# Sliding-window attention with an S4 convolution: the softmax's maximum over eight keys, one reduction in PSUM or three two-operand maxima on a bf16 copy

## The chip, the cores and the metric

The kernel runs on one core of a Trainium2 chip. The metric is the device time of one execution in microseconds (us); lower is better. A profile of one execution gives each engine's instructions with their times, counted from the start of the span. The engines are PE (TensorE, the matmuls; PEld is its weight loads), DVE (VectorE), ACT (ScalarE), POOL (GpSimd) and SP (SyncE, which here issues the DMAs). Each engine works through its own instructions in order and waits on semaphores for the others.

## The reference, cut to what matters

Four layers follow one another on x of shape 1 x 2048 x 512, each added to its own input: attention A, convolution B, attention A, convolution B. The attention has 32 heads of 16 channels, and each position sees only eight keys: itself and those 2, 4, ... 14 positions back.

```python
W, dil = 8, 2
idx = pos[:, None] - off[None, :]          # off = arange(8) * 2
logits = einsum("bhsd,bhswd->bhsw", q, kg) * scale
logits = where(mask, logits, -1e9)         # mask: idx >= 0
attn = softmax(logits, axis=-1)            # over the 8 keys w
o = einsum("bhsw,bhswd->bhsd", attn, vg)
x = x + o.reshape(B, S, D) @ wo            # A, on layernorm(x)
x = x + irfft(rfft(u) * rfft(K)) + u * Dskip   # B, u = layernorm(x); ...
```

The softmax's maximum over the eight keys is what the change touches. Any number near the maximum gives the same softmax up to rounding, since it is subtracted from all eight logits.

## The kernel before

Sequence positions are laid out as 16 rows of 128 partitions (position = 16 p + row), so that a shift by two positions is a shift by two rows. The attention is the method `core` (from L307), called once per attention layer (l = 0 and 1). It has two parts that run into each other.

The **logit part** goes over four blocks q of four rows each and over four quarters ft of the channels. `mult` (L295, DVE) writes the products of q with eight shifted k as prod, 128 x 4096 bf16, in two buffers. `lsum` (L302, PE) sums groups of 16 channels with 32 small matmuls into the PSUM tile L of the block, 128 x (4 rows, 8 keys, 32 heads) in f32; after the last quarter `mask` (L285, PE) adds -1e9 where a key lies ahead of the sequence. L has two buffers. Then the softmax of the block:

- `mx` (L365, DVE): one tensor_reduce over the keys, which reads L from PSUM with the keys as the innermost, strided axis, and writes mx, 128 x 128 bf16.
- `sub_exp` (L372, PE, and L375, ACT): two matmuls with the negative identity subtract mx inside L, and one activation writes ex = exp(scale * L) as 128 x 1024 bf16 to SBUF.
- `recip` (L382, PE; L384 and L386, ACT): sums ex over the keys by eight matmuls, then takes ln and exp(-.) of the sum, giving rs.
- `norm_p` (L392, DVE): attn = ex * rs.

Between these, PE computes the projections `q_proj` (L185) and `v_proj` (L351), which ACT copies out of PSUM (L187 and L353). Once all odd or all even rows of v are there, two DMAs shift them by one partition (L356, L357).

The **PV part** goes over the 16 rows n. `pv_mult` (L402, DVE) writes attn times eight shifted v as pav (128 x 4096 bf16, two buffers); `pv_sum` (L412, PE) sums and transposes it with 64 matmuls into po (one PSUM buffer), which ACT copies to oT (L415); `out_proj` (L424, PE) follows one row later, and ACT writes the new x_sb with its sum (L430) and the sum of its squares (L108, into ln_junk). Each of these two ends in an accumulator read. The layernorm of the next layer is begun and applied in between (L133 to L160). The last block's logits are still made during this part: its four `mult` come after n = 1, 3, 5 and 7, so block 2's maximum falls at n = 0 and block 3's at n = 8.

In layer 0 ACT and DVE also prepare the convolution during the PV part: sines for a table (L700, with a table load before and after, L700 and L1367), and the copies k_perm from k_rl (L1354).

The order on DVE, ACT, PE and SP is the program's own within the attention. The counts n and ft, and a dictionary `ev` keyed by places such as ("p", 8), say where in the loops the other work goes:

```python
for n in range(16):
    pv_mult(rows[n])
    if n in (0, 8):
        mx(2 + n // 8)
    ...
    event(("p", n))
    ...
    pv_sum(rows[n])
    if n in (0, 8):
        sub_exp(2 + n // 8)
```

The convolution is the class FftB: its constant g_sb (1 MB) is loaded by SP (L726), as are the filter's spectra into kf_ring (L795, L797) and kx in its second pass. Its first step is the matmuls L756. These loads stand outside the written order: where they go on SP depends on when the memory that they overlay comes free.

Of the kernel before, what the change touches and what calls it, by code (L numbers as in the profile page):

```python
# [20 lines left out]
P = 128  # L21
# [42 lines left out]
u m UA m u m u m u m u u yD yA u m yA m m u u u m yA m yA  # L64
yA m yD yD yA yD yA yA yA yD z01D z03D yA yA z00D z02D z12D z11A z10D z13B
"""

def build_a_consts(tc, nc, cpool, tpool):
    c = {}
# [93 lines left out]
class LayerA:  # L163
# [125 lines left out]
    def mult(self, q, ft, pr=None):  # L289
        nc, a0, kT = self.nc, q * 4, self.kT  # L290
        if pr is None:
            pr = self.prp.tile([P, W, 4, P], BF16, name="prod")[:]
        kb = kT[:, ft, a0 + 14: a0 + 18, :]
        kap = bass.AP(tensor=kT.tensor, offset=kb.offset, ap=[list(kb.ap[0]), [-2 * P, W], [P, 4], [1, P]])
        nc.vector.tensor_tensor(pr, self.qT[q][:, ft].unsqueeze(1).to_broadcast([P, W, 4, P]), kap, ALU.mult)  # L295
        self.st[q][ft] = pr
# [7 lines left out]
        if ft == NDT - 1:  # L304
            self.mask(q)

    def core(self, x_sb, u, lnp, ev=None, nprod=0):  # L307

        tc, nc, lnst, l = self.tc, self.nc, self.lnst, self.layer
        ident, nident = self.c["ident"], self.c["nident"]  # L310
        scale = float(DH) ** -0.5
        xnT = self.xnT
        ev = ev or {}
        if self.ps_l is None:
            self.open_logits()
        st, linit, mult, lsum = self.st, self.linit, self.mult, self.lsum

        def event(key):
            for f in ev.get(key, ()):
                f()  # L320

        with ExitStack() as c2:
            big = c2.enter_context(tc.tile_pool(name=f"a{l}_big", bufs=1, reuse_waits="tile"))
# [24 lines left out]
            def v_proj(a):  # L348
                pp = pq_tile()
                for dt in range(NDT):  # L350
                    nc.tensor.matmul(pp[:], lhsT=xnT[:, dt, a * P:(a + 1) * P],  # L351
                                     rhs=wv[:, dt, :], start=(dt == 0), stop=(dt == NDT - 1))
                nc.scalar.copy(v[:, 14 + a, :].rearrange("p (d h) -> p d h", h=H), pp[:].rearrange("p (h d) -> p d h", h=H))  # L353
                if a >= 14:
                    b = a - 14
                    nc.sync.dma_start(v[1:113, b:14:2, :], v[0:112, 16 + b:30:2, :])  # L356
                    nc.sync.dma_start(v[113:128, b:14:2, :], v[112:127, 16 + b:30:2, :])  # L357
                    if b + l == 0:
                        self.load_wo(big)
                    event(("v", b))  # L360

            def mx(q):
                L = st[q]["L"]
                m = wk.tile([P, 4, H], BF16, name="mx", bufs=1)
                nc.vector.tensor_reduce(m[:], L[:].rearrange("p a w h -> p a h w"), AX.X, ALU.max)  # L365
                st[q]["mx"] = m

            def sub_exp(q):
                L, m = st[q]["L"], st[q]["mx"]
                ex = wk.tile([P, 4, W, H], BF16, name="ex", bufs=1)  # L370
                for j in range(2):
                    nc.tensor.matmul(L[:, 2 * j:2 * j + 2], lhsT=nident[:],  # L372
                                     rhs=m[:, 2 * j:2 * j + 2].unsqueeze(2).to_broadcast([P, 2, W, H]),
                                     start=False, stop=True, skip_group_check=True)
                nc.scalar.activation(ex[:], L[:], ACT.Exp, scale=scale)  # L375
                st[q]["ex"] = ex

            def recip(q):
                ex, L = st[q]["ex"], st[q]["L"]
# [69 lines left out]
            def u_end(a0):  # L449
                lns[a0] = ln_end(nc, lnp, lns[a0])  # L450

            def u_apply(a0, rows, eng=None):
                rstd, nb = lns[a0]
                for a in rows:
# [2 lines left out]

            nc.sync.dma_start(v[0:1, 0:14, :].rearrange("p a (n c) -> p (a n) c", c=64),
                              self.c["zrow"].unsqueeze(1).to_broadcast([1, 112, 64]))
            projs = [(q_proj, 1, ft) for ft in range(NDT)] if 1 not in self.qT else []  # L460
            vs = [*range(0, NA, 2), *range(1, NA, 2)]
            projs += [(v_proj, a) for a in vs[:6]] + [(q_proj, 2, ft) for ft in range(NDT)]
            projs += [(v_proj, a) for a in vs[6:]]
            slots = [(0, ft) for ft in range(nprod, NDT)] + [(q, ft) for q in (1, 2) for ft in range(NDT)]
            free = 2 if l else 0
            lead = 0 if l else 2
            per, acc = (len(projs) - lead) / (len(slots) - free - 0.5), float(lead)

            def proj(n):
                nonlocal acc  # L470
                acc += n
                while acc >= 1 and projs:
                    f, *args = projs.pop(0)
                    f(*args)
                    acc -= 1

            for q, ft in slots:
                if q == 1 and ft == 0 and 1 not in self.qT:
                    while 1 not in self.qT or projs[0][0] is q_proj:
                        proj(1)  # L480
                event(("m", q, ft))
                mult(q, ft)
                event(("q", q, ft))
                if ft == 0:
                    linit(q)
                if q or ft >= free:
                    proj(per)
                if ft == 0 and q > 0:
                    mx(q - 1)
                lsum(q, ft)  # L490
                if ft == 0 and q > 0:
                    proj(0.5)
                    acc -= 0.5
                    sub_exp(q - 1)
                if ft == 2 and q > 0:
                    recip(q - 1)
                if ft == 3 and q > 0:
                    norm_p(q - 1)
            proj(100)
            linit(3)  # L500
            q_proj(3, 0)
            rows = [0, 2, 1, *range(3, NA)]
            for n in range(16):
                pv_mult(rows[n])
                if n in (0, 8):
                    mx(2 + n // 8)
                if n in (2, 10):
                    recip(2 + n // 8)
                if n in (4, 11):
                    norm_p(2 + n // 8)  # L510
                if n in (1, 3, 5, 7):
                    mult(3, n // 2)
                if n in (7, 11, 15):
                    u_begin(n - 7, n - 3, "act", "act" if n > 7 else "pool")
                if n in (8, 12):
                    u_end(n - 8)
                if n in (9, 10, 13, 14):
                    b0 = 0 if n < 11 else 4
                    r0 = b0 + (0 if n in (9, 13) else 2)
                    u_apply(b0, range(r0, r0 + 2))  # L520
                if n == 15:
                    x_stats(12)
                event(("p", n))
                if n in (1, 3, 5):
                    q_proj(3, n // 2 + 1)
                pv_sum(rows[n])
                if n in (0, 8):
                    sub_exp(2 + n // 8)
                if n == 15:
                    x_stats(13)  # L530
                    if l == 1:
                        u_end(8)
                        u_apply(8, range(8, 12), "dve")
                if n > 0:
                    out_proj(rows[n - 1])
                if n in (1, 3, 5, 7):
                    lsum(3, n // 2)
                event(("o", n))
            if l == 0:
                out_proj(15)  # L540
                return {"a": lambda: [u_end(8), u_apply(8, range(8, 12), "pool")], "s": lambda: x_stats(14), "t": lambda: x_stats(15),
# [744 lines left out]
def kernel(  # L1286
# [74 lines left out]
    with tc.tile_pool(name="ctmp_g2", bufs=1) as g2tmp, tc.manual_schedule(engines=MAN):  # L1361
        gx, gs = build_g2(nc, g2tmp, C["p21"], g2_dram, kp[:].rearrange("p q a r -> p (q a r)"))
        G = lambda f, h: lambda: f(h)
        K = lambda h, j: lambda: k_part(h, j)
        ev = {("v", 0): [lambda: x_load((0,))], ("v", 1): [lambda: x_load((1, 2, 3))], ("o", 1): [lambda: k_half_load(0)], ("o", 2): [G(gs, 0)], 
              ("m", 0, 3): [G(gx, h) for h in range(4)],
              ("p", 3): [G(gs, 1)], ("p", 4): [G(gs, 2)], ("p", 5): [G(gs, 3), lambda: k_half_load(1)], ("o", 5): [lambda: nc.scalar.preload_act_table_set(EXP_LN)],  # L1367
              ("p", 6): [lambda: k_half_fix(0), K(0, 0)], ("p", 7): [K(0, 1)], ("p", 8): [lambda: la.load_w2(w2_dram), K(0, 2)], ("p", 9): [K(0, 3)],
              ("p", 12): [lambda: k_half_fix(1), K(1, 0)], ("p", 13): [K(1, 1), K(1, 2)], ("p", 14): [K(1, 3)]}
        late = la.core(x_sb, u, lnp, ev, 3)  # L1370
    late["m"] = C["masks"]
    krctx2.close()
    la.close_logits()
# [13 lines left out]
    with tc.manual_schedule(engines=MAN):  # L1387
# [33 lines left out]
        fb.c_ps.close()  # L1421
        fb.c_grp.close()
        krctx.close()
        ev = {("p", 8): [lambda: la.load_w2(w2_dram)]}
        ev["m", 0, 0] = [last(("P", 3, 0), ("P", 3, 1), ("x", 0), ("x", 2), ("P", 3, 2), ("Q", 0, 1), ("e", 0), ("Q", 0, 2))]
        ev["m", 0, 1] = [last(("e", 1), ("e", 2))]
        ev["m", 0, 2] = [last(("e", 3))]
        ev["q", 0, 0] = [last(("P", 3, 3), ("Q", 0, 3))]
        la.core(x_sb, u, lnp, ev)
    la.close_logits()  # L1430

    fb = FftB(tc, nc, C, consts["ident"], w2_dram, g2_dram, kf_dram, x_sb, 1)
# [47 lines left out]
```

## Time and profile before

| what | us |
|---|---|
| median of 3 runs | 422.05 |
| lowest and highest | 421.33 and 422.5 |
| the profiled execution's own time | 418.89 |
| its span in the profile | 417.1 |
| logit part of layer 0 and of layer 1, about | 104 to 140 and 276 to 312 |
| PV part of layer 0 and of layer 1, about | 140 to 196 and 312 to 365 |
| second convolution, about | 369 to 417 |

The span is what lies between the first and the last instruction that the profile shows; the execution's own time is 1.79 us longer. A line of a timeline gives the start, the duration, the engine, the source line, the operation, what it writes and reads with shapes, and how many instructions were merged into the line; a bracket at its end gives how long the engine was idle before it and what it waited for. A line of a group gives the count, the busy time in us and the mean of one in ns, and then the idle time before such instructions.

### The profile page before, as it was taken

The numbers are of one execution on the slowest core, as the hardware profiler recorded it, in microseconds if no ns is written. First come the engines' busy times: TensorE is split into PE (matmuls) and PEld (weight loads), VectorE is DVE, ScalarE is ACT, GpSimd is POOL, SyncE is SP. The second block draws the span as 40 slices with busy tenths as digits, with TensorE's granted clock in tenths as the row PEclk, the third lists the DMA queues.
The fourth block names the chain that finished last, engine by engine and source line by source line (L and its number), as shares of the span: only waits on it lengthen the run. The fifth ranks groups of instructions, "written<-read, shape, count | busy, mean of one in ns | idle before, by whom it ended". The sixth has DMA issues, their size and how long they took to land.

```text
span 417.1 us, 15864 instructions
## 1 busy us (share of the span) xinstructions
PE 320.5 (77%) x7048; PEld 231.5 (55%) x7106; DVE 387.9 (93%) x515; ACT 321.7 (77%) x552; POOL 37.7 (9%) x46
## 2 busy tenths in 40 slices
PE   3000068999999987778998779999998978896885
PEld 2000036667756565556887768555665655566774
DVE  8999999999899999996999969979779999989995
ACT  6999998987445569987999998863555758779972
POOL 3000200000396000000500000000000020000000
PEclk9999998999999999999999999999999999999899
DMA  8940642113014666393226597730043027504506
GB/s 222 383 125 13 73 90 71 33 40 89 14 40 123 179 180 189 99 389 109 70 89 229 217 306 218 231 99 2 3 114 89 5 79 328 156 3 140 168 10 197
DMA packets 62462, 54.36 MB, mean 130 GB/s; under 512 B 33877, under 2 KB 50874, under 8 KB 61114
## 3 DMA queue, kind: packets, MB, share of 16 engines
q1 hardware_dynamic: 62250, 53.22, 42.0%
q8 instruction: 55, 0.90, 0.9%
q10 hardware_dynamic: 144, 0.13, 0.1%
q14 instruction: 13, 0.11, 0.1%
HBM read 30.28 MB, written 13.24 MB: 104 GB/s over the span
## 4 chain that ended last, share of the span: by engine, by line
PE 35%; DVE 21%; ACT 14%; issue 5%; DMA 5%; SPq 3%; DVEq 0%; ACTq 0%
PE pq L351 6%; DVE pav L402 5%; DVE t L805 5%; PE L L302 4%; DVE a1s L745 4%; PE pk L1175 4%; PE pq L185 3%; DVE prod L295 3%; PE pp L242 3%; PE po L412 3%; PE pp L1113 3%; PE pq L424 2%; SPq L1280 2%; DMA w_sb<-w_dram 2%; ACT ub L818 1%
## 5 line engine op out<-in xcount | busy, mean ns | idle before, releaser
L402 DVE TENSOR_TENSOR pav<-attn,v_ext 128x4096 bf16<-128x4096 bf16 x32 | 72.8, 2283 | 0.1
L295 DVE TENSOR_TENSOR prod<-qT,kT_ext 128x4096 bf16<-128x4096 bf16 x29 | 66.0, 2299 | 3.9 <-PE L L302 3.8
L412 PE MATMUL po<-ident,pav 64*128 64x64 bf16 x2048 | 36.3, 190 | 15.1 <-DVE pav L402 7.7
L412 PEld LDWEIGHTS <-pav 64*128 64x128 bf16 x2048 | 32.5, 95 | 26.0 <-DVE pav L402 14.9
L1103 PE MATMUL pt<-ident,x_blk 128*128 128x128 bf16 x64 | 7.0, 260 | 43.4 <-ACT x_blk L158 43.4
L1015 DVE TENSOR_TENSOR A_t<-A_t,pow_t 128x1024 bf16<-128x1024 bf16 (+4 forms) x46 | 38.1, 868 | 0.2
L424 PE MATMUL pq<-wop,oT 128*128 128x512 bf16 x121 | 31.7, 379 | 4.3 <-issue 3.8
L353 ACT CAST v_ext<-pq 128x512 bf16<-128x512 f32 x32 | 18.8, 587 | 19.2 <-PE pq L351 17.5
L818 ACT CAST ub<-pb 128x1024 bf16<-128x1024 f32 x32 | 32.2, 1036 | 1.7 <-DVE t L805 0.8
L763 PE MATMUL pb<-a1s,w_sb 128*128 128x64 bf16 x768 | 28.4, 196 | 6.2 <-ACT a1s L745 2.9
L302 PEld LDWEIGHTS <-prod 128*128 128x128 bf16 x928 | 27.0, 96 | 8.1 <-DVE prod L295 2.5
L1103 PEld LDWEIGHTS <-x_blk 128*128 128x128 bf16 x64 | 5.4, 117 | 46.1 <-ACT x_blk L158 44.4
L745 DVE CAST a1s<-pb 128x1024 bf16<-128x1024 f32 x23 | 27.0, 1215 | 3.9 <-PE pb L756 3.9
L763 PEld LDWEIGHTS <-w_sb 128*128 128x128 bf16 x768 | 25.8, 100 | 8.6 <-issue 6.8
L351 PE MATMUL pq<-wv,xnT 128*128 128x512 bf16 x118 | 29.9, 379 | 0.5
L1113 PE MATMUL pp<-xnT,kT_ext 128*128 128x512 bf16 x87 | 25.0, 406 | 6.2 <-ACT qT L1118 3.3
L302 PE MATMUL L<-ind,prod 128*128 128x8 bf16 x928 | 27.4, 166 | 0.8 <-DVE prod L295 0.6
L415 ACT CAST oT<-po 128x512 bf16<-128x512 f32 x32 | 18.5, 577 | 11.5 <-PE po L412 11.2
L745 ACT CAST a1s<-pb 128x1024 bf16<-128x1024 f32 x25 | 24.9, 1034 | 2.5 <-PE pb L756 2.2
L1175 PEld LDWEIGHTS <-A_t 128*64 128x64 bf16 (+1 forms) x512 | 22.3, 105 | 3.6
L1175 PE MATMUL pk<-B_t,A_t 128*64 128x84 bf16 (+1 forms) x512 | 24.1, 203 | 0.1
L832 PE MATMUL pb<-Wp,t 64*128 64x64 bf16 x512 | 19.4, 192 | 5.9 <-ACT ub L818 2.8
(225 smaller groups left out, 809.8 us busy)
## 6 DMA issues: line engine op xcount, KB each, us to landing
w_sb<-w_dram SPq DMA_DIRECT2D x8, 1024.0 KB, 9.4
w_dram<-w_zero SPq DMA_DIRECT2D x1, 4096.0 KB, 14.8
kf_ring<-kf_dram SPq DMA_DIRECT2D x13, 256.0 KB, 3.7
kf_ring<-kf_dram SPq DMA_DIRECT2D x26, 128.0 KB, 3.6
v_ext<-v_ext SPq DMA_DIRECT2D x4, 784.0 KB, 6.2
x_blk<-in_A_x_dram SPq DMA_DIRECT2D x4, 512.0 KB, 4.1
kT_ext<-in_A_wqkv_dram SPq DMA_DIRECT2D x4, 512.0 KB, 10.1
x_sb<-in_A_x_dram SPq DMA_DIRECT2D x4, 512.0 KB, 5.4
```

Of the source, the lines that this page charges most:

```text
L295: nc.vector.tensor_tensor(pr, self.qT[q][:, ft].unsqueeze(1).to_broadcast([P, W, 4, P]), kap, ALU.mult)
L302: self.nc.tensor.matmul(L[:, al, w, ft * 8:(ft + 1) * 8], lhsT=pr[:, w, al, :], rhs=self.c["ind8"][:], start=(ft == 0 and w == 0 and al % ...
L351: nc.tensor.matmul(pp[:], lhsT=xnT[:, dt, a * P:(a + 1) * P], rhs=wv[:, dt, :], start=(dt == 0), stop=(dt == NDT - 1))
L402: nc.vector.tensor_tensor(pv[:], attn[:, n % 4].unsqueeze(2).to_broadcast([P, W, DH, H]), vap, ALU.mult)
L412: nc.tensor.matmul(po[:, h, 0, ft, :], lhsT=pvf[rows, w, ft * P:(ft + 1) * P], rhs=ident[rows, rows], start=(w == 0 and ft == 0), stop=(w ...
L424: nc.tensor.matmul(pw[:], lhsT=oT[:, ftp, :], rhs=self.wo[:, ftp, :], start=False, stop=(ftp == NDT - 1))
L745: (self.nc.scalar.copy if eng == "act" else self.nc.vector.tensor_copy)(dst, src)
L763: nc.tensor.matmul(p2[:, j, :], lhsT=self.w2[:, ec * EC + j, :], rhs=a1s[:, ec * EC + j, :], start=True, stop=True)
L818: nc.scalar.copy(ub[:], p2)
L1015: return lambda: nc.vector.tensor_tensor(*args)
L1113: nc.tensor.matmul(pps[kind, b, ft][:], lhsT=la.wqk[:, dt, c:c + P], rhs=la.xnT[:, dt, b * 512:(b + 1) * 512], start=(dt == 0), stop=(dt = ...
L1175: nc.tensor.matmul(o, lhsT=lhs, rhs=Bt[:, ri, c * CH + ql].rearrange("p b g -> p (b g)"), start=(not half and j % 4 == 0 and ri == 0), sto ...
```

## The change

The maximum is no longer taken from PSUM. A new step `lcopy` has ACT copy the masked logits L to bf16 in SBUF, into the tile that will later hold ex. `mx` then takes the maximum over the keys with three tensor_tensor instructions in place: keys 0 to 3 against 4 to 7 (512 results per partition), then 0 and 1 against 2 and 3 (256), then 0 against 1 (128 results, into mx). `sub_exp` still subtracts mx from the f32 logits in PSUM and still writes ex, over the copy. The tile ex gets two buffers in place of one.

```diff
+            def lcopy(q):
+                L = st[q]["L"]
+                ex = wk.tile([P, 4, W, H], BF16, name="ex", bufs=2)
+                nc.scalar.copy(ex[:], L[:])
+                st[q]["ex"] = ex
 
             def mx(q):
-                L = st[q]["L"]
+                ex = st[q]["ex"]
                 m = wk.tile([P, 4, H], BF16, name="mx", bufs=1)
-                nc.vector.tensor_reduce(m[:], L[:].rearrange("p a w h -> p a h w"), AX.X, ALU.max)
+                for n in (4, 2, 1):
+                    o = ex[:, :, 0:n] if n > 1 else m[:].unsqueeze(2)
+                    nc.vector.tensor_tensor(o, ex[:, :, 0:n], ex[:, :, n:2 * n], ALU.max)
                 st[q]["mx"] = m
 
             def sub_exp(q):
-                L, m = st[q]["L"], st[q]["mx"]
-                ex = wk.tile([P, 4, W, H], BF16, name="ex", bufs=1)
+                L, m, ex = st[q]["L"], st[q]["mx"], st[q]["ex"]
...
                 nc.scalar.activation(ex[:], L[:], ACT.Exp, scale=scale)
-                st[q]["ex"] = ex
```

The loops and events of `core` are replaced by a string for each layer that names one operation per letter, in the order in which they are issued (m mult, l lsum, q and v the projections, c lcopy, x mx, e sub_exp, r recip, n norm_p, P pv_mult, S pv_sum, O out_proj, b, d and a the layernorm, digits and capitals the convolution's preparation):

```diff
+CORE0 = """
+0mvvvvlcmvvxlemqqlmqqlrmvvlcnmvvxlvemvlmvvlrmvvlcnqPxSePmqSOl1PrSO2Pm3qSOlPn4SOPm56qSOl7P8ASOPmb
+BSOlcPxdwCSeOPaaDSOPraaSOPnbSOPd9ESOPaaFGSOPaaHSOPbtStO
+"""
+CORE1 = """
+0m1l2ml3mqqlmqqvlcmvvxlvemvvlmqqlrmqqvlcnmvvxlvemvvlmvvlrmvvlcnqPxSePmqSOlPrSOPmqSOlPnSOPmqSOlPS
+OPmbSOlcPxdwSeOPaaSOPraaSOPnbSOPdSOPaaSOPaaSOPbtStdaaaaO
+"""
```

In the built programs the instructions of PE and POOL stand in the same order before and after. On DVE each tensor_reduce is replaced by three tensor_tensor at its place, and nothing else moves. On ACT each lcopy is put in right after the block's last `lsum` and `mask` in the order of issue: in layer 0 behind the fourth v_ext copy, then between others of them, before the first qT copy of the PV part, and, for block 3, between an accumulator read of ln_junk and a k_perm copy (the letters `lcPxdwC`). On SP the second g_sb load stands behind the kx loads in place of ahead of the ring's first loads, and one pair of ring loads (L797) stands ahead of the first v_ext shift of layer 1 in place of behind it.

More of the change, by code (lines that the diff above doesn't have):

```diff
@@ L66 @@
 """
+CORE0 = """
[6 more added lines that the diff above has]
+"""
+ROWS0 = (0, 2, 1, 3, 4, 5, 6, 7, 8, 9, 10, 11, 12, 13, 14, 15)
+ROWS1 = (0, 2, 1, 3, 4, 5, 6, 7, 8, 9, 10, 11, 12, 13, 14, 15)
+VROWS = (*range(0, 16, 2), *range(1, 16, 2))
 def build_a_consts(tc, nc, cpool, tpool):
@@ L305, in lsum, with core @@
             self.mask(q)
-    def core(self, x_sb, u, lnp, ev=None, nprod=0):
+    def core(self, x_sb, u, lnp, order, ev, nprod=0):
         tc, nc, lnst, l = self.tc, self.nc, self.lnst, self.layer
@@ L312, in core @@
         xnT = self.xnT
-        ev = ev or {}
         if self.ps_l is None:
@@ L316, in core @@
         st, linit, mult, lsum = self.st, self.linit, self.mult, self.lsum
-        def event(key):
-            for f in ev.get(key, ()):
-                f()
         with ExitStack() as c2:
@@ L359, in v_proj @@
                         self.load_wo(big)
-                    event(("v", b))
+                    if ("v", b) in ev:
+                        ev["v", b]()
+            def lcopy(q):
[3 more added lines that the diff above has]
+                st[q]["ex"] = ex
             def mx(q):
-                L = st[q]["L"]
+                ex = st[q]["ex"]
                 m = wk.tile([P, 4, H], BF16, name="mx", bufs=1)
-                nc.vector.tensor_reduce(m[:], L[:].rearrange("p a w h -> p a h w"), AX.X, ALU.max)
+                for n in (4, 2, 1):
+                    o = ex[:, :, 0:n] if n > 1 else m[:].unsqueeze(2)
+                    nc.vector.tensor_tensor(o, ex[:, :, 0:n], ex[:, :, n:2 * n], ALU.max)
                 st[q]["mx"] = m
             def sub_exp(q):
-                L, m = st[q]["L"], st[q]["mx"]
-                ex = wk.tile([P, 4, W, H], BF16, name="ex", bufs=1)
+                L, m, ex = st[q]["L"], st[q]["mx"], st[q]["ex"]
                 for j in range(2):
@@ L459, in core @@
                               self.c["zrow"].unsqueeze(1).to_broadcast([1, 112, 64]))
[L460 to L538, printed above, removed]
@@ new lines, in calls, with logit, g @@
+            def calls(f, *args):
+                return [lambda a=a: f(*a) for a in args]
+            def logit(f):
+                def g(q, ft):
+                    if ft == 0:
+                        linit(q)
+                    f(q, ft)
+                return g
+            qft = [(q, ft) for q in range(4) for ft in range(NDT)]
+            blocks = [(q,) for q in range(4)]
+            rows = [(a,) for a in (ROWS1 if l else ROWS0)]
+            ops = dict(
+                m=calls(mult, *qft[nprod:]), l=calls(logit(lsum), *qft[nprod:]),
+                q=calls(q_proj, *qft[len(self.qT) * NDT:]), v=calls(v_proj, *((a,) for a in VROWS)),
+                x=calls(mx, *blocks), c=calls(lcopy, *blocks), e=calls(sub_exp, *blocks), r=calls(recip, *blocks), n=calls(norm_p, *blocks),
+                P=calls(pv_mult, *rows), S=calls(pv_sum, *rows), O=calls(out_proj, *rows[:15]), t=calls(x_stats, (12,), (13,)),
+                b=calls(u_begin, (0, 4, "act", "pool"), (4, 8, "act", "act"), (8, 12, "act", "act")),
+                d=calls(u_end, (0,), (4,), (8,)),
+                a=calls(u_apply, *((a0, (a,)) for a0 in (0, 4) for a in range(a0, a0 + 4)), *((8, (a,), "dve") for a in range(8, 12))))
@@ L539, in core @@
+            ops = {key: iter(f) for key, f in ops.items()}
+            for c in "".join(order.split()):
+                if c in ev:
+                    ev[c]()
+                else:
+                    next(ops[c])()
+            assert all(next(ops[c], None) is None for c in "mlqvcxernPSOtb")
             if l == 0:
@@ L1364 @@
         K = lambda h, j: lambda: k_part(h, j)
[L1365 to L1370, printed above, removed]
+        ev = {("v", 0): lambda: x_load((0,)), ("v", 1): lambda: x_load((1, 2, 3)),
+              "0": lambda: [gx(h) for h in range(4)], "1": lambda: k_half_load(0), "6": lambda: k_half_load(1),
+              "2": G(gs, 0), "3": G(gs, 1), "4": G(gs, 2), "5": G(gs, 3),
+              "7": lambda: nc.scalar.preload_act_table_set(EXP_LN), "w": lambda: la.load_w2(w2_dram),
+              "8": lambda: k_half_fix(0), "9": lambda: k_half_fix(1)}
+        ev |= {c: K(i // 4, i % 4) for i, c in enumerate("ABCDEFGH")}
+        late = la.core(x_sb, u, lnp, CORE0, ev, 3)
     late["m"] = C["masks"]
@@ L1423 @@
         krctx.close()
[L1424 to L1429, printed above, removed]
+        ev = {"w": lambda: la.load_w2(w2_dram),
+              "0": last(("P", 3, 0), ("P", 3, 1), ("x", 0), ("x", 2), ("P", 3, 2), ("Q", 0, 1), ("e", 0), ("Q", 0, 2)),
+              "1": last(("P", 3, 3), ("Q", 0, 3)), "2": last(("e", 1), ("e", 2)), "3": last(("e", 3))}
+        la.core(x_sb, u, lnp, CORE1, ev)
     la.close_logits()
```

## The prediction

> **What bounds the kernel now.** I read four views: the page's table of busy time, the window view by stage, the groups kept apart by shape, and the timelines of VectorE (DVE), ScalarE (ACT) and TensorE (PE) around the eight maxima. The page first:
>
> ```profile
> PE 320.5 (77%) x7048; PEld 231.5 (55%) x7106; DVE 387.9 (93%) x515; ACT 321.7 (77%) x552; POOL 37.7 (9%) x46
> ```
>
> DVE is 93% busy, so shortening its work looks worth the full amount. That is an average. The window view (stretch, length, then busy time and instruction count of PE, PEld, DVE, ACT, POOL, then clock and DMA) says otherwise for the places of the change:
>
> ```profile
> 120.00:140.00 20.00, 19.79 (x301) 12.56 (x303) 18.91 (x12) 11.23 (x21) 12.05 (x9) 1.00 0.45 119
> 154.00:172.00 18.00, 13.82 (x411) 9.98 (x409) 17.73 (x15) 17.24 (x33) 1.02 (x1) 1.00 0.45 129
> 281.00:314.00 33.00, 32.53 (x471) 20.17 (x477) 27.89 (x17) 16.88 (x30) 0.00 (x0) 1.00 0.14 38
> 343.00:356.00 13.00, 10.54 (x346) 7.40 (x350) 12.96 (x14) 10.13 (x26) 1.08 (x1) 1.00 0.76 309
> ```
>
> In the logit parts (120 to 140 in layer 0, 281 to 314 in layer 1) PE has no gap and DVE has some; there PE sets the pace. In the PV parts DVE is full, and in layer 0 from 154 to 172 ACT is full too (17.24 of 18.00). Now the groups by shape: what goes, and rows for what comes.
>
> ```profile
> L365 DVE TENSOR_REDUCE mx<-L 128x128 bf16<-128x1024 f32 x8 | 9.7, 1218 | 0.8 <-PE L L285 0.8
> L1015 DVE TENSOR_TENSOR A_t<-A_t,pow_t 128x512 bf16<-128x512 bf16 x8 | 3.0, 417 | 0.0
> L1015 DVE TENSOR_TENSOR A_t<-A_t,pow_t 128x256 bf16<-128x256 bf16 x8 | 2.1, 283 | 0.0
> L375 ACT ACTIVATE ex<-L 128x1024 bf16<-128x1024 f32 x8 | 8.2, 1026 | 0.7 <-PE L L372 0.6
> ```
>
> The maxima stand at 119.28, 130.74, 142.11 and 171.76 us (layer 0) and 288.47, 301.61, 314.50 and 343.12 us (layer 1). The fourth of layer 0 decides. Its DVE, ACT and PE timelines:
>
> ```profile
> 169.56 2.29 DVE L402 TENSOR_TENSOR pav<-attn,v_ext 128x4096 bf16<-128x4096 bf16 x1
> 171.76 1.22 DVE L365 TENSOR_REDUCE mx<-L 128x128 bf16<-128x1024 f32 x1
> 172.89 0.16 DVE L148 SCALAR_TENSOR_TENSOR ln_nb<-ln_s,ln_rstd 128x4 f32<-128x4 f32 x1
> ```
>
> ```profile
> 172.07 0.19 ACT L108 ACTIVATION_READ_ACCUMULATOR ln_junk<-x_sb 128x1 f32 x1
> 172.16 1.03 ACT L1354 COPY k_perm<-k_rl 128x1024 bf16<-128x1024 bf16 x1
> 173.10 0.57 ACT L415 CAST oT<-po 128x512 bf16<-128x512 f32 x1
> 173.66 1.02 ACT L375 ACTIVATE ex<-L 128x1024 bf16<-128x1024 f32 x1
> ```
>
> ```profile
> 171.49 0.20 PE L285 MATMUL L<-maskrow,rows 1*128 1x64 bf16 x1
> ```
>
> The mask, the last write to L, ends at 171.69 and DVE reads L at 171.76. ACT comes to the place where the copy is inserted, behind ln_junk's accumulator read and ahead of the k_perm copy, only at 172.16. In layer 1 the same place looks different:
>
> ```profile
> 342.01 0.19 ACT L108 ACTIVATION_READ_ACCUMULATOR ln_junk<-x_sb 128x1 f32 x1
> 344.41 0.59 ACT L415 CAST oT<-po 128x512 bf16<-128x512 f32 x1 [2.22 <-PE po L412]
> ```
>
> Here ACT idles 2.22 us, which is room for a copy.
>
> **What the Trainium skill says.** "VectorE: DVE Perf Modes", The perf-mode tier table: tensor_reduce runs at one element per cycle, a bf16 SBUF tensor_tensor at two, and a PSUM operand loses that. The trace agrees: 1218 ns for 1024 elements reduced, 417 ns for a 512-element bf16 tensor_tensor, and 684 ns for one of 512 in f32. "ScalarE: Activation LUTs", What ACT_TABLE_LOAD costs: an activation with immediates takes 186 + 0.833 N ns and neighbours overlap by about 93 ns; for N = 1024 that is 1039 ns. The exp row has 1026, and 0.94 lies between the starts at 172.16 and 173.10. The same page, Table sets, lists copy in every set, so the copies load no table; the casts beside the table loads here load none either.
>
> **The change part by part.**
>
> *DVE, removed:* eight reduces of 1.22 us. The next instruction starts 1.13 us after one starts (171.76 to 172.89), since neighbours overlap by 0.08.
>
> *DVE, added:* eight trees of 512, 256 and 128 results. The first two rows give 417 and 283 ns; the line through them gives 216 for the third. Each level waits for the one before; a dependent pair (ln_msq at 168.47 for 0.14, ln_veps at 168.64) shows 0.03 us for that. Sum 0.42 + 0.03 + 0.28 + 0.03 + 0.22 = 0.98, less 0.08 of overlap: 0.90. A tree saves 0.23 us, **1.8 us over eight** if nothing else waits. Bounds: at one element per cycle the levels would cost 0.68 + 0.42 + 0.28 (684 for 512, then 417 and 283, a level's count doubled), 1.36 with waits and overlap, a loss of 0.23 each; below, 0.80 if the short levels overlap. I take 0.90, as operands are bf16 with dense inner runs.
>
> *ACT, added:* eight casts of 128x1024 f32, 1.03 us each and 0.94 of queue time; 8.2 us of busy time.
>
> *The wait added:* DVE's tree waits for ACT's copy, which waits for the mask and for all ACT has ahead. Behind the tree on DVE stand the next products; on PE the subtraction (L372) and all that follows it. Place by place, copy end plus 0.04 us for the handover:
>
> - Layer 0, first and second: ACT is at the copy before the mask ends (v_ext ends at 117.2 and 129.55, masks at about 118.6 and 130.05). Copies end near 119.65 and 131.1, trees start 0.4 late and finish 0.1 late. DVE's later idle of 0.37 and 0.72 before attn covers that, and PE, without a gap, has its subtraction later (121.10, 133.38). Cost 0.
> - Layer 1, first and second: copies from 288.5 and 301.6 end near 289.5 and 302.65. The products behind start 0.75 late and end by 292.6 and 305.8; PE takes them up at 293.92 and 307.07. DVE's 0.87 idle there covers it. Cost 0, and none of the DVE saving is gained. If PE ceased to set the pace, each would cost the 0.75.
> - Third of both layers: masks end at 141.37 and 313.75, copies near 142.4 and 314.75. Trees start 0.3 late, run 0.23 shorter: +0.05 to 0.1, on a full DVE. In layer 0 the ACT-bound stretch after hides it; in layer 1 count **+0.05**.
> - Fourth of layer 1: ACT is free at 342.10, the copy ends at 343.13, the tree starts at 343.17 instead of 343.12. Gain 0.18 on DVE; the subtraction follows PE's own po (ends 344.37), so the exp gains nothing. Count **-0.10**.
> - Fourth of layer 0: copy 172.16 to 173.19, tree from 173.23, 1.47 late. Less the 0.23, DVE goes on at 174.1 instead of 172.89, **+1.20**. The subtraction moves as much, and ACT is 0.94 later from the copy and 1.2 from the exp on. With DVE, ACT and PE all moved, nothing is left that keeps the old time, and the delay goes through to the FFT's start at 196.05, where PE comes from the last out_proj.
>
> *SP's queue and buffers:* ex has two buffers, 2 KB more per partition, which moves what lies behind it. In the built program layer 1's g_sb load (1 MB, 250.93 before) waits for the last pav's sum (PE, 363.4), behind the kx loads and ahead of the ring refills of 378.70. It lands 4.9 us after issue by its row, needed near 403. Its traffic meets PE's instruction fetches at the start of the last FFT; in layer 0, where it was issued at 193.89, the weight loads of L756 waited 0.4 for issue. Between 0 and 0.4: **+0.20**. Two ring pieces of 128 KB pass ahead of the v_ext shifts (before: 304.91, now right after 271.79), both long before use at 377 and before ACT's v_ext release: 0. PE's order is the same, POOL's too.
>
> Sum: 1.20 + 0.05 - 0.10 + 0.20 = **+1.35 us**. The profiled execution took 418.89 us (span 417.1 and 1.79 around it), so 420.24 there; the median of the three runs is 422.05, 3.16 above the profile, so **423.4**.
>
> **Rivals.**
>
> 1. *DVE is the bound everywhere and copies arrive in time:* the full 1.8 us is gained, 420.25. For it: 93% busy. Against it: PE's gapless stretches and ACT at 172.16. It decides if the fourth copy of layer 0 ends before 171.76, that is, if ACT gets there 1.4 us earlier; ACT's backlog would have to shrink, and nothing does that. Chance 0.10.
> 2. *Absorbed:* PE lost 0.83 at 182.31 and 0.92 at 188.50 to instruction issue while w_sb was loading. If these gaps end at a fixed time, a later PE falls into them with less loss; the last pav ended at 191.89 and its sum began at 192.75, so DVE has 0.86 of slack there. Layer 0 then costs 0.4: 422.5. Chance 0.16.
> 3. *Trees at one element per cycle, or more lost to ACT:* 0.46 more on each of the four late maxima is 1.8, and up to 0.94 if ACT's extra cast is not overlapped by the stall: 425 to 426. Chance 0.22.
>
> Main case 0.52. Its own range is 422.6 to 424.2. A change of 0.3% (1.27 us) is about what a measurement can tell from none; the main case lies on that line and I split it 0.30 slower, 0.22 same. Slower 0.30 + 0.22 = 0.52, same 0.22 + 0.16 = 0.38, faster 0.10. Leaving out rival 1 and the upper end of 3: 421.1 to 425.2.
>
> **What would show it.** Right: DVE idle of about 1.4 us before the fourth tree of layer 0, released by the ACT cast; next to none at the fourth of layer 1; trees near 0.98 us; FFT start about 1.2 later than 196.05; the stretch 281 to 314 of unchanged length. Wrong: no such wait, a tree above 1.3 us, new PE idle in the logit parts, or ring products waiting for a DMA after 377.

## The result and the profile after

The changed kernel took 423.75 us (median of 20 runs, 420.87 to 425.90) and the kernel before 420.99 us (20 runs). The ratio is 1.0058, 95% interval 1.0038 to 1.0078. A second series gave 423.25 against 421.52 us, 1.0029 (1.0006 to 1.0051). The ratios on record are not quotients of these medians, which are 1.0066 and 1.0041. So the change costs about 0.3 to 0.6%.

From the page after, the table of busy time:

```profile
PE 329.3 (78%) x7106; PEld 232.3 (55%) x7106; DVE 388.1 (92%) x531; ACT 329.5 (78%) x560; POOL 38.0 (9%) x46
```

ACT has 7.8 us more, near the 8.2 forecast for eight copies. DVE has no less: 388.1 us against 387.9. The groups by shape of after:

```profile
L374 ACT CAST ex<-L 128x1024 bf16<-128x1024 f32 x8 | 8.1, 1007 | 3.3 <-PE L L298 3.3
...
L382 DVE TENSOR_TENSOR ex<-ex 128x512 bf16<-128x512 bf16 x8 | 3.4, 424 | 7.1 <-ACT ex L374 7.1
L382 DVE TENSOR_TENSOR ex<-ex 128x256 bf16<-128x256 bf16 x8 | 3.0, 374 | 0.3
L382 DVE TENSOR_TENSOR mx<-ex 128x128 bf16<-128x128 bf16 x8 | 2.5, 310 | 0.3
```

The trees sum to 8.9 us of busy time where the reduces had 9.7; this 0.8 us does not show in DVE's total, in part because the products prod took 66.6 us in place of 66.0. The first level has about the 417 ns of the row in the prediction, but in the mean the second and third are dearer than the 283 and 216 ns assumed, and DVE waited 7.1 us for the copies. In the timeline of DVE, the fourth tree of layer 0 (the instructions of two levels are merged in its first line):

```profile
174.63 0.75 DVE L382 TENSOR_TENSOR ex<-ex 128x512 bf16<-128x512 bf16 x2 [2.43 <-ACT ex L374]
175.42 0.23 DVE L382 TENSOR_TENSOR mx<-ex 128x128 bf16<-128x128 bf16 x1
```

And of ACT at that place:

```profile
173.51 0.19 ACT L121 ACTIVATION_READ_ACCUMULATOR ln_junk<-x_sb 128x1 f32 x1
173.61 0.99 ACT L374 CAST ex<-L 128x1024 bf16<-128x1024 f32 x1
```

The tree starts 0.03 us after the copy ends, and the copy starts as soon as ACT is through with ln_junk. This is the wait that the prediction named, but it is 2.43 us, not 1.4. The window view of after says what else happened in this one execution:

```profile
160.00:164.00 4.00, 4.00 (x59) 1.76 (x59) 4.00 (x2) 3.29 (x7) 0.00 (x0) 0.63 0.93 272
```

The TensorE clock granted there was 0.63 (1.00 before), and PE, and ACT behind it, came late. The profile of the second series (e1 below) has a clock of 1.00 from 140 to 172, and there the wait is 1.35 us.

### The profile page after: what moved, and what is told of

The parts are those of the page before. It is cut to its first block, busy times and chain, and to the rows that moved or that the text cites. A ratio compares the mean times of both kernels' runs of the same rounds, so it can differ in the third digit from the quotient of the medians.

```text
span 422.4 us, 15938 instructions
## 1 busy us (share of the span) xinstructions
PE 329.3 (78%) x7106; PEld 232.3 (55%) x7106; DVE 388.1 (92%) x531; ACT 329.5 (78%) x560; POOL 38.0 (9%) x46
## 4 chain that ended last, share of the span: by engine, by line
PE 39%; DVE 22%; ACT 11%; DMA 6%; issue 5%; SPq 1%; DVEq 0%; ACTq 0%
DVE pav L417 5%; PE pq L359 5%; PE pk L1139 5%; DVE prod L308 5%; DVE a1s L709 4%; PE po L427 4%; PE pp L1077 4%; PE L L315 3%; DVE t L769 3%; PE pq L439 3%; PE pp L255 3%; PE pq L198 2%; PE pb L796 2%; DMA kf_ring<-kf_dram 2%; ACT ub L782 1%
## 5 line engine op out<-in xcount | busy, mean ns | idle before, releaser
L308 DVE TENSOR_TENSOR prod<-qT,kT_ext 128x4096 bf16<-128x4096 bf16 x29 | 66.6, 2324 | 0.2
L439 PE MATMUL pq<-wop,oT 128*128 128x512 bf16 x128 | 33.8, 387 | 0.0
L1077 PE MATMUL pp<-xnT,kT_ext 128*128 128x512 bf16 x96 | 26.6, 405 | 5.7 <-ACT qT L1082 2.8
L709 DVE CAST a1s<-pb 128x1024 bf16<-128x1024 f32 x23 | 27.1, 1218 | 3.6 <-PE pb L720 3.6
L198 PE MATMUL pq<-xnT,kT_ext 128*128 128x512 bf16 x96 | 24.1, 387 | 0.0
```

What stands on the lines that cost most here:

```text
L439: nc.tensor.matmul(pw[:], lhsT=oT[:, ftp, :], rhs=self.wo[:, ftp, :], start=False, stop=(ftp == NDT - 1))
L709: (self.nc.scalar.copy if eng == "act" else self.nc.vector.tensor_copy)(dst, src)
L1077: nc.tensor.matmul(pps[kind, b, ft][:], lhsT=la.wqk[:, dt, c:c + P], rhs=la.xnT[:, dt, b * 512:(b + 1) * 512], start=(dt == 0), stop=(dt = ...
```

## The experiments

Three theories could explain the loss. **W**: the loss is the fourth tree of layer 0, which waits for ACT's backlog. **C**: the dips of the clock, which the profile of after has and that of before hasn't, are chance and explain no loss. **M**: the second buffer of ex moves other buffers and the g_sb load, and that is the loss. Later came **Q**: ACT's added queue time is the loss, whether DVE waits or not. All ratios are to the kernel before, timed on the same chip in five rounds; the first four share one series of before (421.52 us), the next four another (421.08 us), the last four a third (420.91 us).

### e1: the changed kernel again

> The changed kernel once more, to see what of its profile repeats. Theory W (the wait of the fourth tree of layer 0 on ScalarE's copy makes the loss): DVE idle of 1.2 to 2.5 us before that tree again, the stretch from the fourth prod of layer 0's last block to the FFT longer by 1.2 to 2.3 us than before, and a ratio near 1.0045 to 1.006. Theory C (the profile of the changed kernel caught stretches in which PE's clock was granted at about 0.6, at 160 to 164 us and at 347 to 351, and these are chance): in this profile those stretches lie elsewhere, the wait is about 1.4 us, and the convolution of layer 0 is not 1.9 us longer. Theory M (the moved buffers and SP's moved loads cost): the stretch from the last pav of layer 1 to the second convolution is longer by 0.3 to 1 us again.

Measured: 423.25 us, 1.0029 (1.0006 to 1.0051). The timeline of DVE, then of ACT, in e1:

```profile
173.23 0.75 DVE L382 TENSOR_TENSOR ex<-ex 128x512 bf16<-128x512 bf16 x2 [1.35 <-ACT ex L374]
174.01 0.22 DVE L382 TENSOR_TENSOR mx<-ex 128x128 bf16<-128x128 bf16 x1
174.16 0.15 DVE L161 SCALAR_TENSOR_TENSOR ln_nb<-ln_s,ln_rstd 128x4 f32<-128x4 f32 x1
```

```profile
172.20 0.99 ACT L374 CAST ex<-L 128x1024 bf16<-128x1024 f32 x1
173.09 1.04 ACT L1318 COPY k_perm<-k_rl 128x1024 bf16<-128x1024 bf16 x1
...
175.41 1.02 ACT L391 ACTIVATE ex<-L 128x1024 bf16<-128x1024 f32 x1 [0.79 <-PE L L388]
```

ln_nb, which follows the maximum, starts at 174.16, in the profile of before at 172.89: 1.27 later. The exp starts 1.75 later (175.41 against 173.66), the last k_perm copy of this part at 190.67 against 188.96, and the FFT's first matmul at 197.76 against 196.05: ACT is 1.71 us late at the end of the stage. Of this 0.43 is chance: the clock from 172 to 180 was 0.79, and the subtraction took 1.03 us where it takes 0.60 at full clock. W and C hold. M's sign is there as well: from the end of layer 1's last pav to the second convolution's first matmul it is 7.27 us, before 6.72, within the 0.3 to 1 us expected.

### e2 and e3: the buffers

```diff
-                ex = wk.tile([P, 4, W, H], BF16, name="ex", bufs=2)   # e2, in the kernel after
+                ex = wk.tile([P, 4, W, H], BF16, name="ex", bufs=1)
-                ex = wk.tile([P, 4, W, H], BF16, name="ex", bufs=1)   # e3, in the kernel before
+                ex = wk.tile([P, 4, W, H], BF16, name="ex", bufs=2)
```

> The changed kernel with one buffer for ex, as before; SP's order, the g_sb load and the placing of the tiles are then those of the kernel before, and no copy should have to wait for the one buffer, since attn of the block before has been made by then. Theory W: as the changed kernel, ratio 1.004 to 1.006. Theory M: the part due to the layout goes, 0.2 to 1 us, and the ratio falls to 1.001 to 1.004. Theory C: as the changed kernel within noise.

> The kernel before with two buffers for ex and nothing else: it has the reduce and SP's moved g_sb and ring loads. Theory W: same as before, ratio 0.999 to 1.001. Theory M: slower by 0.2 to 1 us or more, 1.0005 to 1.003.

Measured: e2, with g_sb issued early again (255.65), 423.38 us, 1.0045 (1.0018 to 1.0073), with the same wait of 1.35 us. e3, the reduces with two buffers of ex, 420.99 us, 0.9984 (0.9964 to 1.0004); its g_sb load is issued at 366.31 as after, not at 250.93. So the loss comes without the moved load, and the moved load comes without a loss. M falls as an account of the loss.

The second buffer does change the schedule, though, where the prediction did not look: in the logit part of layer 0. In the kernel before, the first product that DVE writes to prod has to wait for PE:

```profile
114.87 4.49 DVE L295 TENSOR_TENSOR prod<-qT,kT_ext 128x4096 bf16<-128x4096 bf16 x2 [2.07 <-PE L L302]
```

With two buffers this wait is gone (first product at 112.84 in e3), and from PE's first logit sum of layer 0 to the first pav it takes 31.51 us in e3 and 32.26 before. In e1, which has both the second buffer and the trees, it is 32.33. PE in e3, then in e1:

```profile
120.24 0.59 PE L372 MATMUL L<-mx,nident 128*128 128x512 bf16 x2
```

```profile
120.61 0.61 PE L388 MATMUL L<-mx,nident 128*128 128x512 bf16 x2 [0.28 <-DVE mx L382]
...
134.63 0.95 PE L315 MATMUL L<-ind,prod 128*128 128x8 bf16 x32 [0.23 <-DVE prod L308]
```

So here the second buffer gains 0.75 us and the first two trees lose 0.8. In after and in e4, e5, e7, e9 and e10, which have both, the stretch is within 0.02 us of e1's; e2, with trees and one buffer, has 32.77, 0.5 more than before.

### e4 and e6: the fourth block of layer 0 alone, and all but it

The string of a layer leaves out the letter c of a block that keeps the reduce. In e4 this is block 3 of layer 0 (shown), in e6 it is the other seven blocks:

```diff
-BSOlcPxdwCSeOPaaDSOPraaSOPnbSOPd9ESOPaaFGSOPaaHSOPbtStO
+BSOlPxdwCSeOPaaDSOPraaSOPnbSOPd9ESOPaaFGSOPaaHSOPbtStO
...
+                if ex is None:
+                    nc.vector.tensor_reduce(m[:], L[:].rearrange("p a w h -> p a h w"), AX.X, ALU.max)
```

> The changed kernel, but block 3 of layer 0 alone takes its maximum by the reduce from PSUM, with no copy; the other seven keep copy and tree. Theory W: the loss is in this block, so the ratio falls to 0.999 to 1.002 and DVE has no idle before that maximum. Theory M or a loss spread over all eight places: the ratio stays at 1.003 to 1.006.

> Copy and tree in block 3 of layer 0 alone; the other seven maxima are the reduce of the kernel before. W: the whole loss is here, idle of 1.3 to 1.5 us before that tree, ratio 1.002 to 1.005. If the loss were spread over the seven others: ratio 0.999 to 1.001.

Measured: e4 420.73 us, 0.9981 (0.9959 to 1.0003). e6 422.06 us, 1.0021 (0.9993 to 1.0048). Seven trees and the second buffer, without the fourth tree of layer 0, show no loss. That tree alone has most of the loss in its point estimate, though its interval still holds no loss. e6 has reduces at the first two places and so the 0.75 us gain of e3 (its stretch is 31.51 as well); against e3, an estimate from the two ratios, it is 1.0037 times as long.

Both waits missed what was expected. DVE in e4, then in e6:

```profile
173.01 1.23 DVE L382 TENSOR_REDUCE mx<-L 128x128 bf16<-128x1024 f32 x1 [1.02 <-PE L L299]
```

```profile
173.92 0.75 DVE L385 TENSOR_TENSOR ex<-ex 128x512 bf16<-128x512 bf16 x2 [2.50 <-ACT ex L375]
```

In e4 no idle time was expected, and DVE waited 1.02 us, for PE's mask and not for a copy; in e6 it waited 2.50 us, not 1.3 to 1.5. Both profiled executions had a slow clock ahead of this place, e4 0.60 from 158 to 162 and e6 0.58 from 150 to 154. So a late PE alone can hold the fourth maximum up by 1 us, with no copy in the way.

### e5 and e9: the copy earlier in ACT's order

Only the order of the letters at row 7 is changed. The diff is e5's; in e9 the line begins with BlcSOP:

```diff
-BSOlcPxdwCSeOPaaDSOPraaSOPnbSOPd9ESOPaaFGSOPaaHSOPbtStO
+BSlcOPxdwCSeOPaaDSOPraaSOPnbSOPd9ESOPaaFGSOPaaHSOPbtStO
```

> The kernel after with, in block 3 of layer 0 alone, lsum and lcopy ordered ahead of row 7's out_proj, so that ACT's copy stands right behind oT of row 7 and ahead of x_sb and ln_junk, and PE's last logit sums stand ahead of that out_proj. Theory W (the loss is the fourth tree of layer 0, which waits for ACT's backlog): the copy then ends near or before the time DVE comes free, the idle before the tree falls from 1.35 us to under 0.4, and the ratio to the kernel before is 0.998 to 1.001. Theory Q (ACT's added 0.94 us in a stretch where ACT is full is the loss, whether DVE waits or not): the idle goes but the ratio stays at 1.002 to 1.005. Theory M (moved buffers and loads): ratio stays at 1.003.

> One step further than the copy ahead of out_proj: in block 3 of layer 0, lsum and lcopy stand ahead of row 7's pv_sum too, so that PE makes the last logit sums in the time in which it waits for oT, and ACT's copy stands ahead of that row's oT. W: the copy ends near 171.7, the time at which DVE comes free, idle before the tree under 0.3 us, ratio to the kernel before 0.996 to 1.000. Q (the added ACT time is the loss whether DVE waits or not): ratio 1.002 to 1.004.

Measured: e5 421.32 us, 1.0005 (0.9985 to 1.0025), and DVE still waited 0.93 us, not under 0.4 as expected. ACT, then PE, in e5:

```profile
171.65 1.01 ACT L374 CAST ex<-L 128x1024 bf16<-128x1024 f32 x1 [0.40 <-PE L L298]
```

```profile
169.48 1.11 PE L427 MATMUL po<-ident,pav 64*128 64x64 bf16 x64 [1.37 <-ACT oT L430]
```

ACT was free, but PE had made the last sums only after row 7's pv_sum, which had waited 1.37 us for oT. Up to that pv_sum e5 has the order of e1, where it stands earlier:

```profile
168.52 1.11 PE L427 MATMUL po<-ident,pav 64*128 64x64 bf16 x64 [0.87 <-ACT oT L430]
```

DVE's product ahead of the tree starts at 169.48 in e5 and 169.59 in e1, so PE was about 1.07 us later against DVE in e5. The clock of this execution was 0.59 from 158 to 162, as in e4. Without that, an estimate from these starts, the copy would have ended near 171.59 in place of 172.66, ahead of the 171.76 at which DVE came free: the 0.93 us are probably chance, and e5's order may be enough.

In e9 the last sums stand ahead of row 7's pv_sum; ACT, then DVE, in e9:

```profile
169.71 1.01 ACT L374 CAST ex<-L 128x1024 bf16<-128x1024 f32 x1
170.76 0.59 ACT L430 CAST oT<-po 128x512 bf16<-128x512 f32 x1
...
175.76 1.02 ACT L391 ACTIVATE ex<-L 128x1024 bf16<-128x1024 f32 x1
```

```profile
171.75 0.74 DVE L382 TENSOR_TENSOR ex<-ex 128x512 bf16<-128x512 bf16 x2
172.53 0.22 DVE L382 TENSOR_TENSOR mx<-ex 128x128 bf16<-128x128 bf16 x1
```

The copy ends at 170.72, the tree starts at 171.75 with no idle time ahead of it, and ln_nb follows at 172.68, 0.21 earlier than before. e9 took 420.52 us, 0.9991 (0.9969 to 1.0013): with all eight copies and trees in place no loss is left to be seen. It is also no gain that could be told from nothing. The exp stands at 175.76, later than in e1 (175.41): a late exp does not make the loss by itself.

### e7 and e10: is it the wait, or ACT's longer queue?

```diff
                 m = wk.tile([P, 4, H], BF16, name="mx", bufs=1)
+                if (l, q) == (0, 3):                     # e7 and e10
+                    L = st[q]["L"]
+                    nc.vector.tensor_reduce(m[:], L[:].rearrange("p a w h -> p a h w"), AX.X, ALU.max)
...
-                nc.scalar.copy(ex[:], L[:])
+                nc.scalar.copy(ex[:], L[:] if (l, q) != (0, 3) else st[2]["ex"][:])   # e10
```

> The kernel after, but in block 3 of layer 0 DVE takes the maximum by the reduce from PSUM, while ACT still makes the copy, which nothing reads. DVE no longer waits for ACT there; ACT's queue is as long as after. W: the reduce starts with no idle from ACT, ratio 0.998 to 1.001. Q: the added 0.94 us of ACT's queue is the loss, ratio 1.002 to 1.004. Both parts as the prediction has them (1.2 on DVE and PE, 0.94 on ACT): in between, 1.001 to 1.002.

> Repairs the run with the copy kept: there the built program let the reduce wait for ACT's copy, as both read the PSUM tile L, so DVE waited all the same. Here, in block 3 of layer 0, ACT's copy takes the ex of block 2 as its source (a copy of the same size, which nothing reads), and DVE's reduce of L waits for the mask alone. W: no idle released by ACT, ratio 0.998 to 1.001. Q: 1.002 to 1.004. Both, as the prediction has it (0.94 us of ACT's queue counts as well): 1.001 to 1.002.

Measured: e7 422.95 us, 1.0041 (1.0021 to 1.0061). It did not test what it was meant to; the timeline of DVE in e7:

```profile
173.70 1.23 DVE L382 TENSOR_REDUCE mx<-L 128x128 bf16<-128x1024 f32 x1 [1.35 <-ACT ex L374]
```

In the built program the reduce waits for ACT's copy, though both only read L. So e7 is a second case of the wait, with the old instruction behind it: wait kept, loss kept. e10 gives ACT a copy of another tile, and DVE and ACT there read:

```profile
172.01 1.22 DVE L382 TENSOR_REDUCE mx<-L 128x128 bf16<-128x1024 f32 x1
```

```profile
172.41 1.03 ACT L374 COPY ex<-ex 128x1024 bf16<-128x1024 bf16 x1
173.35 1.04 ACT L1321 COPY k_perm<-k_rl 128x1024 bf16<-128x1024 bf16 x1
...
174.77 1.02 ACT L394 ACTIVATE ex<-L 128x1024 bf16<-128x1024 f32 x1
```

The exp is 2.76 us behind the start of the reduce (before: 1.90), so ACT's 0.86 us is there, and the time is 420.77 us, 0.9997 (0.9969 to 1.0024). ACT's queue time alone costs nothing that can be told; its interval leaves up to 1 us open. e9, which keeps the copy of L on ACT, says the same. Q falls as the main cause.

### e8 and e11: trees that wait for nothing

e8 puts the three-level tree on a tile of zeros in the kernel before, filled by POOL; e11 lets the first level read ident, a constant of the kernel:

```diff
-                nc.vector.tensor_reduce(m[:], L[:].rearrange("p a w h -> p a h w"), AX.X, ALU.max)
+                ex = wk.tile([P, 4, W, H], BF16, name="ex", bufs=1)                      # e11
+                idb = ident[:].rearrange("p (a h) -> p a h", h=H).unsqueeze(2).to_broadcast([P, 4, 4, H])
+                for n in (4, 2, 1):
+                    o = ex[:, :, 0:n] if n > 1 else m[:].unsqueeze(2)
+                    nc.vector.tensor_tensor(o, idb if n == 4 else ex[:, :, 0:n], idb if n == 4 else ex[:, :, n:2 * n], ALU.max)
```

> The kernel before with each reduce replaced by the three-level tree on a tile of zeros in SBUF: no copy on ACT, no wait for L; it leaves out the maximum (zero is subtracted). It shows what the shorter work on DVE is worth by itself. The prediction: DVE's 0.23 per tree counts only for the late four maxima, some of which are hidden by ACT; gain 0 to 0.8 us, ratio 0.998 to 1.000. Rival 1 (DVE is the bound everywhere): gain 1.8 us, ratio 0.9957. A tree takes 0.98 us if nothing disturbs it, and the first two of layer 0 take about 1.65 if POOL's work beside them is what slowed them after.

> Repairs the run with trees on zeros, where filling the tile of zeros stood behind POOL's other work and held DVE up for 4.3 us. Here the first level of each tree reads a tile that lies ready since the start (ident), the other two levels and the write of mx are as after. No copy, no wait for L; it leaves out the maximum (0 or 1 is subtracted). Prediction: the shorter DVE work gains 0 to 0.8 us, ratio 0.998 to 1.000. Rival 1 (DVE is the bound everywhere): 8 x 0.23 = 1.8 us, ratio 0.9957.

Measured: e8 423.58 us, 1.0062 (1.0037 to 1.0087, six runs), and void for the question: the filling stood behind POOL's work, and DVE waited for it:

```profile
121.94 1.24 DVE L369 TENSOR_TENSOR zz<-zz 128x512 bf16<-128x512 bf16 x2 [4.31 <-POOL zz L334]
```

e11: 420.64 us, 0.9993 (0.9976 to 1.0011). The shorter work of DVE, freed of copies and waits, is worth 0.3 us (a gain of up to 1.0 or a loss of up to 0.5). This is net of layer 0's logit part, which is 0.5 us longer than before (32.74 against 32.26), since the first two trees were slow here too. Rival 1's 1.8 us, a ratio of 0.9957, is outside.

### e12: no maximum at all

```diff
-                nc.vector.tensor_reduce(m[:], L[:].rearrange("p a w h -> p a h w"), AX.X, ALU.max)
...
-                for j in range(2):
-                    nc.tensor.matmul(L[:, 2 * j:2 * j + 2], lhsT=nident[:],
...
```

> The kernel before without the maximum and its subtraction: exp is taken of the plain logits, which gives the same softmax as long as no exp overflows; the protection against overflow is left out. DVE has eight reduces of 1.13 us less (9.0 us), PE sixteen matmuls less (about 0.6 us a pair, 4.9 us). Rival 1 (DVE is the bound everywhere): 9 us less, ratio 0.978. By stages: PE sets the pace in the logit parts, so its two pairs in each count there (2.4 us), and of the four late maxima DVE's 1.13 us each, some of it hidden: 3 to 6 us less, ratio 0.986 to 0.993.

Measured: 418.43 us, 0.9945 (0.9911 to 0.9980), a gain of 2.3 us (0.8 to 3.8); 3 to 6 were expected. 9 us less work on DVE and 4.9 on PE brought a quarter of the former. Each logit part is shorter by less than 1 us (layer 1's from its first prod to its first pav: 35.28 us against 36.15), and then DVE meets a transfer that had been in time. DVE in layer 0 and in layer 1 of e12:

```profile
147.03 4.49 DVE L396 TENSOR_TENSOR pav<-attn,v_ext 128x4096 bf16<-128x4096 bf16 x2 [1.33 <-DMA v_ext<-v_ext]
...
318.42 4.49 DVE L396 TENSOR_TENSOR pav<-attn,v_ext 128x4096 bf16<-128x4096 bf16 x2 [0.65 <-DMA v_ext<-v_ext]
```

This is the only version whose interval lies below the time of the kernel before, and it does without the protection against overflow; for logits of any size it is no replacement.

**All together.** In five series DVE's fourth maximum of layer 0 waits for ACT's late copy: 1.0058 and 1.0029 (the changed kernel and e1, the same program), 1.0045 (e2), 1.0021 (e6) and 1.0041 (e7), mean 1.0039. In five it waits for no copy: 0.9984 (e3), 0.9981 (e4), 0.9991 (e9), 0.9997 (e10) and 0.9993 (e11), mean 0.9989. e5, with a wait of 0.93 us, has 1.0005. None of the first five lies below any of the others. The closest comparison is of those that share the second buffer and the first three trees: 1.0058, 1.0029 and 1.0041 with the wait, 0.9981 (e4), 0.9991 (e9) and 0.9997 (e10) without; the means are 0.0053 or 2.2 us apart. This is larger than the 1.3 to 1.7 us that the traces of before and e1 show from the wait to the FFT's start, and whether the remainder is more than the scatter of such series was not settled. Single traces cannot settle it: e4, without a copy, took 57.67 us from layer 0's first pav to the FFT, e1 57.89 and the kernel before 56.14, each with its own dips of the clock or none.

## Why the prediction was right, step by step

Forecast were 423.4 us and a loss of 1.35; measured were 423.75 and 423.25 us, losses of 2.8 and 1.7 us against the medians of before (2.4 and 1.2 by the ratios). That the time was met within 0.4 us is in part luck: the forecast started from 422.05, the median of three runs, and 20 runs of the same kernel gave 420.99. The forecast ratio, 1.0032, lies in the interval of the second series and below that of the first. The main step was right, and two others were wrong by about as much in opposite directions.

- **The late copy, +1.20.** Right. ACT came to the copy at 172.20 (forecast 172.16), the tree began at 173.23 (forecast 173.23), and DVE went on at 174.16 (forecast 174.1). The delay then reached the FFT, as stated: in e1 it starts 1.71 us later, 0.43 of that from a slow clock, which leaves about 1.3. By which engine the delay got there is not shown.
- **ACT "0.94 later from the copy".** It is so in the trace, but e10 shows that this part alone costs nothing measurable. Nor does the time of the exp decide: counted from layer 0's first pav it starts at 35.53 us in e1, and at 35.95 in e5 and 35.98 in e9, which show no loss. What goes with the loss is DVE's wait for the late copy; why the late exp of e5 and e9 did not cost was not tested.
- **The price of a tree, 0.98 us.** Right for six of eight (e1: 173.23 to 174.23, 1.00 us). The first two of layer 0 took 1.76 and 1.66 us, which no step foresaw; "a tree above 1.3 us" was one of the prediction's own signs of being wrong. They stand beside POOL's index work. DVE, then POOL, in e1:

```profile
118.80 1.12 DVE L382 TENSOR_TENSOR ex<-ex 128x512 bf16<-128x512 bf16 x2 [1.21 <-ACT ex L374]
120.03 0.53 DVE L382 TENSOR_TENSOR mx<-ex 128x128 bf16<-128x128 bf16 x1
```

```profile
118.03 1.08 POOL L659 IOTA g_i<- 128x512 int32 x2
119.09 1.39 POOL L660 TENSOR_SCALAR g_i<-g_i,aux 128x512 int32<-128x512 int32 x2
```

- **Layer 0, first and second, "cost 0".** Wrong, and hidden. The first pav stands at 139.88 in e1 and at 139.91 before, as if the trees had cost nothing. But e3, with the second buffer and no trees, is 0.8 us faster over this stretch than e1, and PE waits 0.28 and 0.23 us there in e1 where it waits for nothing in e3: the "new PE idle in the logit parts" that the prediction also named as a sign of being wrong.
- **Layer 1, first and second: waits, but cost 0.** Right. DVE's waits in after are

```profile
293.64 0.75 DVE L382 TENSOR_TENSOR ex<-ex 128x512 bf16<-128x512 bf16 x2 [1.70 <-ACT ex L374]
...
306.75 0.75 DVE L382 TENSOR_TENSOR ex<-ex 128x512 bf16<-128x512 bf16 x2 [1.22 <-ACT ex L374]
```

  against 0.61 and 0.17 for the mask before, and the stretch keeps its length: from the first prod to the first pav 36.15 us in both. In e1 the stretch that answers to 281 to 314 of before (2.38 later) has the same 32.53 us and 471 matmuls on PE:

```profile
283.38:316.38 33.00, 32.53 (x471) 20.17 (x477) 27.25 (x21) 18.98 (x33) 0.00 (x0) 1.00 0.11 30
```

- **Third and fourth of layer 1, +0.05 and -0.10.** Right in sign and near in size: counted from the first pav, the third maximum ends at 3.53 us in e1 and 3.42 before, the fourth at 31.96 and 32.04. The fourth waits for nothing; DVE and ACT in after:

```profile
347.35 0.75 DVE L382 TENSOR_TENSOR ex<-ex 128x512 bf16<-128x512 bf16 x2
```

```profile
346.32 0.99 ACT L374 CAST ex<-L 128x1024 bf16<-128x1024 f32 x1
349.42 0.59 ACT L430 CAST oT<-po 128x512 bf16<-128x512 f32 x1 [2.10 <-PE po L427]
```

- **SP's queue and buffers, +0.20.** Not borne out: e3 has the second buffer and the moved load and shows no cost (0.9984). The second buffer's gain of 0.75 us in layer 0's logit part was not foreseen. What the moved load costs by itself is not shown: from the end of the last pav to the second convolution e3 took 7.43 us and before 6.72, but e12, with the load issued early, took 7.29.
- **Rival 1** fell with e11. **Rival 2** (absorbed in PE's gaps of issue) was seen only in part: before its two gaps had 0.83 and 0.92 us, in e1 0.16 and 0.65, but PE then waited longer for oT (0.73 where it had been 0.35), and the FFT was late all the same. **Rival 3**, dearer trees on each of the four late maxima, is not what happened: the late trees took 1.00 us, and two early ones were dearer, beside POOL.

## What to carry to other kernels

Splitting a reduction into cheaper steps on another engine's copy moves its start from "when the data is there" to "when the other engine gets round to it". Read what that engine has queued ahead of the copy at each place, and put the copy into its order where it is idle or early: here two letters moved in the order took the loss away. Before that, ask what the shorter work can be worth, by a version without the copies and waits: here the estimate was 0.3 us, less than one late copy cost.

An unchanged time at the end of a stage does not show that nothing in it changed. Here a gain from a second buffer and a loss from slow trees hid each other, and only a version with one of the two told them apart.

## What the runs showed of the hardware

A tensor_tensor with both inputs in SBUF was slowed where POOL worked on SBUF beside it, and a tensor_reduce from PSUM at the same places was not. In e1 the third level took up to 596 ns where its median is 226, and the tree 1.76 us where it takes 1.00, while before the reduces at the same two places took 1218 and 1210 ns, with POOL's TENSOR_SCALAR running beside both. The Trainium skill, "SBUF — State Buffer", Who interferes with whom, states that a DVE instruction with two SBUF inputs contends with a GpSimd instruction that reads SBUF, and that a tensor_reduce does not. The traces agree in kind: in e1 the first level of the first tree stood mostly beside POOL's IOTA, which reads no tile, and took 427 ns, and the two levels beside TENSOR_SCALAR took 664 and 527. Not every overlap slows, though: the first level of the second tree ran beside TENSOR_SCALAR and took 413 ns. The prediction had not taken this into account.

The clock granted to TensorE fell for a few us in single executions (0.63 from 160 to 164 in after, 0.60 from 158 to 162 in e4, 0.79 from 172 to 180 in e1) and was 1.00 there in others. A wait read from one execution carries this: 2.43 us in one, 1.35 in another, and 1.02 in e4 where no copy was waited for.
